# Linear attention and a gated product on one core: the projection of the last six d_ff tiles of the first token chunk in three float32r products

## The chip, the cores and the metric

The kernel runs on one core of a Trainium2 chip. The metric is the device time of one execution in microseconds, given as the median of several runs. The kernel before takes 996.69 us (three runs, 996.67 to 998.06). Smaller is better.

## What is computed

Attention without a score matrix, then a gated product of two linear layers and an output projection, all in float32:

```
q_s = softmax(q over the 64 head dims);  k_s = softmax(k over the 576 positions)
kv  = k_s^T v            (64 x 64 for each of 8 batches and 8 heads)
x   = q_s kv             (4608 tokens x 512)
out = ((x w_a) * (x w_b)) w_out      (w_a, w_b 512 x 1536, w_out 1536 x 512)
```

## The kernel before, in words

The 4608 tokens are nine chunks of T = 512. d_ff = 1536 is NF = 12 tiles of 128. Weights arrive in HBM as 64-bit words and `to_float` (L85 to L105) makes float32 of them on the chip: two ScalarE passes (L97, L98), one VectorE shift (L100), one GpSimd add (L101), one VectorE merge (L102). The result lies in one of eight buffers `wy`.

Matmuls are exact enough only if each float32 operand is written as a sum of two float32r values: `split` (L74 to L80) has ScalarE cast the source into `hi` (L77) and VectorE subtract `hi` from the source into `lo` (L80). A product then is three float32r matmuls: hi with hi, hi with lo, lo with hi.

**The first chunk (c = 0)** runs in the loop at L550 to L564, one pass for each d_ff tile f. A pass issues the loads of tile f + 3 (`load_f`), the conversion of tile f + 2 (`convert_f`: two halves of w_a and w_b, then w_out), one step of the attention of the next chunk (`attend`), then `gate_first` for tile f and the projection of tile f - 1. `gate_first` (L369 to L387) makes two PSUM tiles of 12 float32r matmuls each (L378), has ScalarE copy the first to `ga` (L385) and VectorE multiply it by the second (L386). `project_first` (L408 to L413) multiplies `ga` by w_out in plain float32: four matmuls of 128x512 (L410), which the profile shows as eight records. The float32 w_out that it reads sits in the half of `wo` that will hold `lo`; `convert_wo` (L122 to L127) brings it there with a DMA from `wy` on SP's queue (L126).

**The later chunks (c = 1 to 8)** run a seven-product scheme on 2x2 blocks (L401) and project with `project` (L415 to L423): 12 float32r matmuls of 128x512 for a tile (L420). They need w_out as hi and lo, which `split_wo` (L129) makes, in place, of the float32 copy; it is called in chunk 1 (L603, L604). The last tile of chunk 0 is projected from `run_pending` inside chunk 1.

**The order of the work.** The program order above is only the order in which the instructions are given. When the program is built, a scheduler simulates it and lays down for each engine a fixed sequence, in which an instruction can run far earlier or later than its place in the source; on the chip every engine and SP's DMA queue work their sequence in order. So the casts and subtractions of `split_wo` are not all found in chunk 1.

The edge between chunk 0 and chunk 1 matters below. Chunk 1 needs the attention output of its last head pair: PE transposes q (`pq`, L316), ScalarE and VectorE split it into `qh` and `ql` (L77, L80), PE makes `px` (L333), ScalarE copies it to `xf` (L472), VectorE and ScalarE make the operands `xt`, `xo` (L351, L77, L80), and only then can `ky` and `ka` (L401) begin.

Of the kernel before, what the change touches and what calls it, by code (L numbers as in the profile page):

```python
# [7 lines left out]
F32 = mybir.dt.float32  # L8
# [21 lines left out]
def linear_attention_then_gated_ffn(  # L30
# [17 lines left out]
    nc = tc.nc  # L48
    B, NP, P, J, _, D = k.shape
# [4 lines left out]
    T = 512  # L54
    H = T // 2
    TT = T // P
    NCH = NT // T

    const = ctx.enter_context(tc.tile_pool(name="const", bufs=1))
    sb = ctx.enter_context(tc.tile_pool(name="sb", bufs=2))  # L60
# [13 lines left out]
    def split(hi, lo, src, hi_engine="act"):  # L74

        if hi_engine == "act":
            nc.scalar.copy(out=hi, in_=src)  # L77
        else:
            nc.vector.tensor_copy(out=hi, in_=src)
        nc.vector.tensor_tensor(out=lo, in0=src, in1=hi.bitcast(F32), op=ALU.subtract)  # L80


    wo = {}

    def to_float(raw):  # L85

        top = raw.bitcast(F32).rearrange("p (n t) -> p n t", t=2)[:, :, 1]
        low = raw.bitcast(U32).rearrange("p (n t) -> p n t", t=2)[:, :, 0]
        y = sb.tile([P, DM], F32, name="wy", bufs=8)
        r = sb.tile([P, DM], I32, name="wr", bufs=4)
        u = raw.bitcast(I32)[:, 0:DM]
        nc.scalar.activation(out=y, in_=top, func=AF.Copy, scale=2.0 ** -112)  # L97
        nc.scalar.activation(out=r, in_=low, func=AF.Copy, scale=2.0 ** -29)  # L98
        yi = y.bitcast(I32)
        nc.vector.tensor_single_scalar(u, yi, 3, op=ALU.logical_shift_left)  # L100
        nc.gpsimd.tensor_tensor(out=r, in0=u, in1=r, op=ALU.add)  # L101
        nc.vector.scalar_tensor_tensor(  # L102
            out=yi, in0=yi, scalar=-(2 ** 31), in1=r, op0=ALU.bitwise_and, op1=ALU.bitwise_or
        )
        return y  # L105
# [3 lines left out]
    def load_f(f):  # L109

        i, r = divmod(f, 2)
        for half in range(2):
            raw = sb.tile([P, DM], I64, name="raw", tag="xo", bufs=11)
            ins = nc.sync.dma_start(out=raw, in_=w_ab[i, r, half])
            raws[f, half] = raw
        raw = const.tile([P, DM], I64, name=f"wo{f}_raw", tag=f"wo{f}")
        with tc.issue_after(ins.ins):
            nc.sync.dma_start(out=raw, in_=w_out[f])
        raws[f, "o"] = raw
        return ins  # L120

    def convert_wo(f):  # L122

        y = to_float(raws.pop((f, "o")))
        w = const.tile([P, 2, DM], F32R, name=f"wo{f}_w", tag=f"wo{f}")
        nc.sync.dma_start(out=w[:, 1].bitcast(F32), in_=y)  # L126
        wo[f] = w  # L127

    def split_wo(f):  # L129
        split(wo[f][:, 0], wo[f][:, 1], wo[f][:, 1].bitcast(F32))  # L130


    def ws_tile():
# [32 lines left out]
    def sums(i):  # L166

        a = {}
        for r in range(2):
            for h in range(2):  # L170
                a[r, h] = sb.tile([P, DM], F32, name="ws_y", tag="wy", bufs=8)
                nc.sync.dma_start(out=a[r, h], in_=dy[i, r, h])
        sub, add = ALU.subtract, ALU.add
        for o, x, y, op in (
            ((1, 1), (1, 0), (1, 1), add),
            ((1, 0), (0, 0), (1, 0), sub),
            ((0, 0), (1, 1), (0, 0), sub),
            ((0, 1), (0, 1), (0, 0), sub),
        ):
            nc.gpsimd.tensor_tensor(out=a[o], in0=a[x], in1=a[y], op=op)  # L180
        return {S1: a[1, 1], S3: a[1, 0], S2: a[0, 0], S4: a[0, 1]}
# [161 lines left out]
    def x_operands(xf, which, box):  # L343

        b11, b12 = xf[:, 0:2, 0:H], xf[:, 0:2, H:T]
        b21, b22 = xf[:, 2:4, 0:H], xf[:, 2:4, H:T]
        for op in which:
            if op == T2:
                t1, t2 = t_tile(), t_tile()
                nc.vector.tensor_tensor(out=t1, in0=b12, in1=b11, op=ALU.subtract)  # L350
                nc.vector.tensor_tensor(out=t2, in0=b22, in1=t1, op=ALU.subtract)  # L351
                box["t1"], box["t2"] = t1, t2
                src = t2
            elif op == T3:
                src = t_tile()
                nc.vector.tensor_tensor(out=src, in0=b22, in1=b12, op=ALU.subtract)
            elif op == T1:
                src = box["t1"]
            elif op == T4:
                src = box["t2"]  # L360
                nc.vector.tensor_tensor(out=src, in0=b21, in1=src, op=ALU.subtract)
            else:
                src = {B11: b11, B21: b21, B22: b22}[op]
            o = xo_tile([P, 2, 2, H])
            split(o[:, 0], o[:, 1], src)
            box[op] = o


    def gate_first(f, x):  # L369

        pp = []
        for n in range(2):
            pt = ps.tile([P, T], F32, name=f"pt{n}", tag=f"k{n}")
            i = 0
            for g in range(NP):
                w = blocks[f, g // 2][:, n, :, g % 2]
                for wp, xp in ((0, 0), (0, 1), (1, 0)):
                    nc.tensor.matmul(  # L378
                        pt, w[:, wp], x[g][:, xp], start=(i == 0), stop=(i == 3 * NP - 1)
                    )  # L380
                    i += 1
            pp.append(pt)
            if n == 0:
                ga = sb.tile([P, T], F32, name="ga", tag=f"gh{f % 2}", bufs=1)
                nc.scalar.copy(out=ga, in_=pt)  # L385
        nc.vector.tensor_tensor(out=ga, in0=pp[1], in1=ga, op=ALU.mult)  # L386
        return ga  # L387

    def g_split(f, g):
        gh = sb.tile([P, T], F32R, name=f"gh{f % 2}", bufs=1)  # L390
        gl = sb.tile([P, T], F32R, name=f"gl{f % 2}", bufs=1)
        split(gh, gl, g)
        return gh, gl
# [14 lines left out]
    def project_first(f, g, po):  # L408
        for t in range(TT):
            nc.tensor.matmul(  # L410
                po[t], g[:, t * P:(t + 1) * P], wo[f][:, 1].bitcast(F32),
                start=(f == 0), stop=(f == NF - 1),
            )  # L413

    def project(f, ghl, po):  # L415
        gh, gl = ghl
        for t in range(TT):
            ts = slice(t * P, (t + 1) * P)
            for i, (a, w) in enumerate(((gh, 0), (gh, 1), (gl, 0))):
                nc.tensor.matmul(  # L420
                    po[t], a[:, ts], wo[f][:, w],
                    start=(f == 0 and i == 0), stop=(f == NF - 1 and i == 2),
                )  # L423

    def store(c, po):
        for t in range(TT):
            ot = sb.tile([P, DM], F32, name="ot", tag="wr", bufs=4)
            if c == NCH - 1:
                nc.scalar.copy(out=ot[:, 0:H], in_=po[t][:, 0:H])
                nc.vector.tensor_copy(out=ot[:, H:], in_=po[t][:, H:])  # L430
            else:
                nc.scalar.copy(out=ot, in_=po[t])
            nc.sync.dma_start(out=out[c * T + t * P:c * T + (t + 1) * P, :], in_=ot)
# [83 lines left out]
    def convert_f(f):  # L517
        convert_ab(f, 0)
        convert_ab(f, 1)
        convert_wo(f)  # L520
# [27 lines left out]
    po = [ps.tile([P, DM], F32, name=f"po{t}") for t in range(TT)]  # L548
    pending = None
    for f in range(NF):  # L550
        for n in range(2, 4) if f == 0 else (f + 3,):
            if n < NF:
                last_load = load_f(n)
        if f + 2 < NF:
            convert_f(f + 2)
        if f:
            attend()
        if f == NF - 1:
            sy[0] = sums(0)
            x_operands(xfs[1], early + late, xo)  # L560
        ghl = gate_first(f, x0)
        if pending is not None:
            project_first(*pending, po)
        pending = (f, ghl)  # L564
    pend = [(pending[0], pending[1], 0, po)]

    def run_pending(last_only=False):

        if not pend:
            return  # L570
        f, ghl, c, po = pend.pop(0)
        (project if c else project_first)(f, ghl, po)
        if f == NF - 1:
            store(c, po)

    for c in range(1, NCH):
        more = c + 1 < NCH
        attend = Spread(attention_tasks(c + 1) if more else [], 3 * NI - 3)
        po = None
        x, xo = xo, {}  # L580
        for i in range(NI):
# [15 lines left out]
            u2 = sb.tile([P, 2, H], F32, name="u2", bufs=1)  # L597
# [13 lines left out]
            if more and i == NI - 1:  # L611
                x_operands(xfs[c + 1], late, xo)
            end = c == NCH - 1 and i == NI - 1
            if not end:
                run_pending()
# [11 lines left out]
            if po is None:  # L627
                po = [ps.tile([P, DM], F32, name=f"po{t}") for t in range(TT)]
# [60 lines left out]
```

## Time and profile before

| | |
|---|---|
| median of the runs | 996.69 us |
| the profiled execution's own time | 995.74 us |
| its span | 993.3 us |
| PE busy | 962.1 us (97%) |
| VectorE busy | 654.0 us (66%) |
| ScalarE busy | 333.5 us (34%) |
| granted TensorE clock, mean | 0.991 |

The span is the stretch from the first to the last instruction; 2.4 us of the execution lie around it. In the rows, PE is TensorE's matmuls, PEld its weight loads, DVE is VectorE, ACT ScalarE, POOL GpSimd, SPq SP's DMA queue. A line number is the line of the kernel before. A helper such as `split` has one line for all its callers, so tile names (`wo_w`, `gh`, `ws`, `ql`) tell them apart. Matmul records overlap, so pitches are read from the chain of work rather than from the mean duration of a record.

### The profile page before, as it was taken

What the parts mean: (1) busy time and instruction counts of PE and PEld (TensorE: products, weight loads), DVE (VectorE), ACT (ScalarE), POOL (GpSimd) and SP (SyncE); (2) the same over time, 40 slices, a digit from 0 to 9 for tenths busy, and PEclk for the clock granted to TensorE, in tenths of its full rate; (3) what the DMA queues carried; (4) which work ended last, traced back from release to release, by engine and by line L of the source; (5) the groups of instructions that cost most, each with busy time, mean ns of one, the idle gap of its engine ahead of it and who ended that gap; (6) DMA issues with size and microseconds to landing.
All of it is one profiled execution on the core that took longest, in us unless ns stands there. A gap on an engine that the chain in (4) does not pass through costs nothing.

```text
span 993.3 us, 16580 instructions
## 1 busy us (share of the span) xinstructions
PE 962.1 (97%) x6276; PEld 866.0 (87%) x6276; DVE 654.0 (66%) x1280; ACT 333.5 (34%) x667; POOL 114.2 (11%) x96
## 2 busy tenths in 40 slices
PE   4889999999999999999999999999999999999998
PEld 4667666999989999999999999999999999999996
DVE  7797887887787774677468656865577555353433
ACT  7666675332342322233223212322233232121111
POOL 3344345440000000000000000000000000000000
PEclk9799998999999999999999999999999999999999
DMA  9599858978777587866796679767867676767761
GB/s 345 216 413 401 336 213 282 384 276 294 239 272 270 212 292 270 292 220 240 239 331 228 229 249 325 257 219 245 296 221 250 211 274 216 251 238 271 252 207 50
DMA packets 84605, 261.35 MB, mean 263 GB/s; under 512 B 9392, under 2 KB 9520, under 8 KB 84528
## 3 DMA queue, kind: packets, MB, share of 16 engines
q1 hardware_dynamic: 84528, 260.31, 73.8%
q8 instruction: 50, 0.82, 0.3%
q14 instruction: 27, 0.22, 0.1%
HBM read 219.38 MB, written 37.75 MB: 259 GB/s over the span
## 4 chain that ended last, share of the span: by engine, by line
PE 83%; DVE 4%; DMA 4%; issue 3%; ACT 2%; POOL 2%; SPq 0%; POOLq 0%; DVEq 0%; ACTq 0%
PE po L420 26%; PE ka L401 14%; PE kx L401 14%; PE kp L401 14%; PE ky L401 7%; PE pk L249 3%; PE px L333 2%; POOL wr L101 2%; PE pt L378 2%; PE po L410 1%; DMA wo_w<-wy 1%; PE pq L316 1%; DMA wo_raw<-in_w_out 1%; DVE ws L80 1%; DMA qt<-in_q 1%
## 5 line engine op out<-in xcount | busy, mean ns | idle before, releaser
L420 PE MATMUL po<-wo_w,gh 128*128 128x512 f32 x768 | 225.0, 394 | 1.0 <-ACT gh L77 1.0
L401 PE MATMUL kx<-xo,ws 128*128 128x256 f32 x1152 | 167.1, 285 | 0.0
L401 PE MATMUL ka<-xo,ws 128*128 128x256 f32 x1152 | 161.9, 285 | 0.2 <-ACT xo L77 0.2
L420 PEld LDWEIGHTS po<-wo_w,gh 128*128 128x128 f32 x768 | 138.4, 189 | 26.6 <-ACT gh L77 1.4
L401 PE MATMUL kp<-xo,ws 128*128 128x256 f32 x1152 | 157.4, 284 | 0.0
L401 PEld LDWEIGHTS kx<-xo,ws 128*128 128x128 f32 x1152 | 152.4, 191 | 4.0 <-ACT ws L77 0.2
L401 PEld LDWEIGHTS ka<-xo,ws 128*128 128x128 f32 x1152 | 151.3, 192 | 4.3 <-ACT xo L77 0.7
L401 PEld LDWEIGHTS kp<-xo,ws 128*128 128x128 f32 x1152 | 147.2, 191 | 1.6
L420 PE MATMUL po<-wo_w,gl 128*128 128x512 f32 x384 | 136.8, 397 | 0.0
L77 ACT CAST gh<-cc 128x512 fp32r<-128x512 f32 x96 | 58.7, 622 | 159.1 <-DVE cc L632 113.1
L631 DVE TENSOR_TENSOR cc<-kp,u 128x512 f32<-128x512 f32 x48 | 33.0, 687 | 82.3 <-PE kp L401 81.9
L420 PEld LDWEIGHTS po<-wo_w,gl 128*128 128x128 f32 x384 | 71.1, 189 | 14.8
L401 PE MATMUL ky<-xo,ws 128*128 128x256 f32 x576 | 80.1, 288 | 1.0 <-ACT xo L77 1.0
L378 PE MATMUL pt<-xo,ws 128*128 128x512 f32 x288 | 74.1, 406 | 3.9 <-ACT ga L385 3.2
L401 PEld LDWEIGHTS ky<-xo,ws 128*128 128x128 f32 x576 | 73.8, 194 | 1.6 <-ACT xo L77 1.4
L80 DVE TENSOR_TENSOR gl<-cc,gh 128x512 fp32r<-128x512 f32 x96 | 68.0, 714 | 10.1 <-ACT gh L77 10.1
L622 ACT COPY cc<-kx 128x256 f32<-128x256 f32 x48 | 17.9, 372 | 168.3 <-PE kx L401 162.9
L621 DVE TENSOR_TENSOR cc<-kp,u 128x512 f32<-128x512 f32 x48 | 33.0, 688 | 62.2 <-PE kp L401 61.9
L378 PEld LDWEIGHTS pt<-xo,ws 128*128 128x128 f32 x288 | 53.3, 188 | 20.3 <-ACT ga L385 4.6
L217 POOL PARTITION_ALL_REDUCE mx<-m x20 | 14.7, 733 | 475.1 <-DVE m L203 434.8
L410 PE MATMUL po<-wo_w,ga 128*128 128x512 f32 x96 | 43.5, 592 | 0.0
L635 DVE TENSOR_TENSOR cc<-ka,u 128x512 f32<-128x512 f32 x48 | 32.9, 685 | 15.4 <-PE ka L401 15.2
(119 smaller groups left out, 1211.0 us busy)
## 6 DMA issues: line engine op xcount, KB each, us to landing
ws<-dw SPq DMA_DIRECT2D x312, 512.0 KB, 4.7
dw<-ws SPq DMA_DIRECT2D x42, 512.0 KB, 4.7
raw<-in_w_ab SPq DMA_DIRECT2D x24, 512.0 KB, 7.9
out<-ot SPq DMA_DIRECT2D x36, 256.0 KB, 4.1
vt<-in_v SPq DMA_DIRECT2D x28, 325.0 KB, 6.1
qt<-in_q SPq DMA_DIRECT2D x32, 256.0 KB, 4.0
kt<-in_k SPq DMA_DIRECT2D x24, 320.0 KB, 4.6
wo_raw<-in_w_out SPq DMA_DIRECT2D x12, 512.0 KB, 8.1
```

Source lines behind the costliest of these rows:

```text
L77: nc.scalar.copy(out=hi, in_=src)
L80: nc.vector.tensor_tensor(out=lo, in0=src, in1=hi.bitcast(F32), op=ALU.subtract)
L101: nc.gpsimd.tensor_tensor(out=r, in0=u, in1=r, op=ALU.add)
L249: nc.tensor.matmul(pk, kt[:, j].rearrange("p h d -> p (h d)"), vt[:, j], start=(j == 0), stop=(j == J - 1),)
L333: nc.tensor.matmul(px[:, s], w, m[:, s], start=(i == 0), stop=(i == 2))
L378: nc.tensor.matmul(pt, w[:, wp], x[g][:, xp], start=(i == 0), stop=(i == 3 * NP - 1))
L401: nc.tensor.matmul(pt[:, n], w[:, n, wp, c], x[:, xp, c], start=(first and n == 0 and i == 0), stop=(i == 5), skip_group_check=True,)
L410: nc.tensor.matmul(po[t], g[:, t * P:(t + 1) * P], wo[f][:, 1].bitcast(F32), start=(f == 0), stop=(f == NF - 1),)
L420: nc.tensor.matmul(po[t], a[:, ts], wo[f][:, w], start=(f == 0 and i == 0), stop=(f == NF - 1 and i == 2),)
L621: nc.vector.tensor_tensor(out=cc[:, 3], in0=kp, in1=u3, op=ALU.add)
L631: nc.vector.tensor_tensor(out=cc[:, 1], in0=kp, in1=u2, op=ALU.add)
L635: nc.vector.tensor_tensor(out=cc[:, 2], in0=ka, in1=u2, op=ALU.add)
```

## The change

With F0 = 6, tiles f = 6 to 11 of the first chunk go another way. Their w_out is split straight from `wy` when it is converted, so there is no float32 copy and no DMA for it; `split_wo` does nothing for them. Their gate result goes into a buffer shared with `u2` and is then split with `g_split` into `gh` and `gl`; their projection is `project`, three float32r products, in place of `project_first`. Tiles 0 to 5 stay as they were.

```diff
+    F0 = 6
...
         y = to_float(raws.pop((f, "o")))
         w = const.tile([P, 2, DM], F32R, name=f"wo{f}_w", tag=f"wo{f}")
-        nc.sync.dma_start(out=w[:, 1].bitcast(F32), in_=y)
+        if f < F0:
+            nc.sync.dma_start(out=w[:, 1].bitcast(F32), in_=y)
+        else:
+            split(w[:, 0], w[:, 1], y)
         wo[f] = w
 
     def split_wo(f):
-        split(wo[f][:, 0], wo[f][:, 1], wo[f][:, 1].bitcast(F32))
+        if f < F0:
+            split(wo[f][:, 0], wo[f][:, 1], wo[f][:, 1].bitcast(F32))
...
             if n == 0:
-                ga = sb.tile([P, T], F32, name="ga", tag=f"gh{f % 2}", bufs=1)
+                ga = sb.tile([P, T], F32, name="ga", tag=f"gh{f % 2}" if f < F0 else "u2", bufs=1)
                 nc.scalar.copy(out=ga, in_=pt)
         nc.vector.tensor_tensor(out=ga, in0=pp[1], in1=ga, op=ALU.mult)
-        return ga
+        return ga if f < F0 else g_split(f, ga)
...
         if pending is not None:
-            project_first(*pending, po)
+            (project_first if pending[0] < F0 else project)(*pending, po)
         pending = (f, ghl)
...
         f, ghl, c, po = pend.pop(0)
-        (project if c else project_first)(f, ghl, po)
+        project(f, ghl, po)
```

## Rows read from the trace of the kernel before

**Rows 1.** The page: busy time by engine, and two of the costliest groups.
```profile
PE 962.1 (97%) x6276; PEld 866.0 (87%) x6276; DVE 654.0 (66%) x1280; ACT 333.5 (34%) x667; POOL 114.2 (11%) x96
...
L77 ACT CAST gh<-cc 128x512 fp32r<-128x512 f32 x96 | 58.7, 622 | 159.1 <-DVE cc L632 113.1
...
L80 DVE TENSOR_TENSOR gl<-cc,gh 128x512 fp32r<-128x512 f32 x96 | 68.0, 714 | 10.1 <-ACT gh L77 10.1
```

**Rows 2.** Busy time of each engine in four stretches; first column the stretch, then its length.
```profile
95.00:147.00 52.00, 50.84 (x198) 34.85 (x197) 42.52 (x69) 35.01 (x85) 22.41 (x16) 1.00 0.73 280
147.00:157.00 10.00, 10.00 (x42) 7.17 (x41) 4.59 (x8) 3.90 (x9) 6.15 (x5) 1.00 0.86 310
157.00:177.00 20.00, 17.54 (x78) 12.69 (x77) 19.20 (x30) 11.90 (x21) 10.41 (x7) 0.83 0.85 300
161.00:263.00 102.00, 98.97 (x673) 90.43 (x671) 85.59 (x161) 37.73 (x67) 29.48 (x20) 0.97 0.86 309
```

**Rows 3.** Who waited for whom, engine PE, 90 to 178 us.
```profile
PE px L333 <- DVE ql L80: 1.7, 2, 0.9
PE ky L401 <- ACT xo L77: 1.0, 1, 1.0
PE pm L208 <- ACT xf L472: 0.7, 1, 0.7
```

**Rows 4.** The chain that ended last, 126 to 172 us: start, length, what.
```profile
137.57 3.43 PE po L410 x8
...
156.76 3.43 PE po L410 x8
...
164.35 0.60 DVE wo_w L80
...
165.48 0.69 DVE ql L80
...
166.21 1.23 PE px L333 x6
...
169.48 0.58 PE ky L401
```

**Rows 5.** The same chain in chunk 1, 188 to 200 us.
```profile
191.97 3.72 PE po L420 x16
```

**Rows 6.** The tile wo_w, 90 to 170 us: durations min/median/max in ns, first and last start.
```profile
L80 DVE TENSOR_TENSOR wo_w<-wo_w x9: 642/679/692, 95.5 to 166.7; 128x512 fp32r<-128x512 f32 x9
L77 ACT CAST wo_w<-wo_w x8: 604/614/626, 99.2 to 148.4; 128x512 fp32r<-128x512 f32 x8
L126 SPq DMA_DIRECT2D wo_w<-wy x6: 471/476/476, 95.8 to 144.0; - x6
...
DMA to landing us min/median/max: 2.3/4.2/7.5
```

**Rows 7.** Groups by line and shape, engine DVE, 95 to 147 us.
```profile
L80 DVE TENSOR_TENSOR ws<-wy,ws 128x512 fp32r<-128x512 f32 x10 | 12.0, 1201 | 2.1 <-ACT ws L77 2.1
...
L80 DVE TENSOR_TENSOR wo_w<-wo_w 128x512 fp32r<-128x512 f32 x6 | 4.0, 675 | 0.0
```

**Rows 8.** The timeline of DVE and PE: the last weight split, an idle time, tile 11's gate.
```profile
145.01 1.53 DVE L80 TENSOR_TENSOR ws<-wy,ws 128x512 fp32r<-128x512 f32 x1
...
154.20 0.69 DVE L299 TENSOR_REDUCE qst<-qt 128x8 f32<-128x512 f32 x1 [3.13 <-DMA qt<-in_q]
...
149.78 4.21 PE L378 MATMUL pt<-xo,ws 128*128 128x512 f32 x16
```

**Rows 9.** Busy time by stretch at the edge of chunk 0; third number from the end the clock.
```profile
168.00:170.00 2.00, 0.85 (x2) 0.43 (x2) 1.92 (x4) 1.24 (x4) 0.00 (x0) 0.62 0.94 357
170.00:172.00 2.00, 1.98 (x10) 1.92 (x10) 2.00 (x6) 1.78 (x5) 0.00 (x0) 0.50 1.04 412
172.00:174.00 2.00, 2.00 (x11) 2.00 (x11) 2.00 (x5) 1.05 (x2) 0.84 (x1) 0.50 1.05 410
174.00:176.00 2.00, 2.00 (x14) 2.00 (x13) 2.00 (x4) 0.22 (x1) 1.92 (x2) 0.68 1.04 400
```

## The prediction, made before the changed kernel was run

> **What bounds the kernel now.** I began with the page's busy times [rows 1]: PE is busy 97% of the span, so PE is the first suspect everywhere. Since an average hides stages, I then read the busy times of the stages that the change touches [rows 2]. From 95 to 147 us, where tiles 6 to 10 are gated, PE is busy 50.84 of 52 us; DVE is busy 42.52, so 9.48 us of it are idle. From 157 to 177 us, the edge between the first and the second chunk, the picture turns: DVE is busy 19.20 of 20 us and PE only 17.54. After the edge PE is the bound again (98.97 of 102 us, chunk 1).
>
> The waits of PE [rows 3] say the same in another way. From 90 to 178 us PE loses 1.7 us in two waits for `ql`, 1.0 for `xo` and 0.7 for `xf`, nearly all of it at the edge, and almost nothing before. The chain of work that ended last [rows 4] shows what such a wait hangs on: the last head pair's `ql` runs at 165.48 us right behind other DVE work, a w_out subtraction at 164.35 among it; `px` follows at 166.21 and `ky` at 169.48. So a microsecond of PE work saved before about 165 us arrives at the end only if this chain moves forward with it.
>
> **The change part by part.**
>
> *The product, on the path.* A plain float32 projection takes 3.43 us for its eight records [rows 4]. In chunk 1, 16 float32r records of the same 128x512 take 3.72 us, 0.2325 each [rows 5], so the twelve of `project` take 2.79 us. That is 3.43 - 2.79 = 0.64 us less for a tile, and for tiles 6 to 11 it is 6 x 0.64 = 3.8 us off PE, all of it in stretches where PE is the bound (the first of the six runs after 119 us, the last right before the edge's `px`).
>
> *The gate split, added.* Six casts of 0.62 us on ACT and six subtractions of 0.71 us on DVE [rows 1]. A projection comes one whole gate and one other projection later than its own gate (24 and 12 records of 0.23 us, 5.5 + 2.8 us), and the added multiply-cast-subtract chain is 0.7 + 0.62 + 0.71, about 2 us, plus its queueing; I cost the latency at nothing, hidden by the next gate. If DVE and ACT queues ate those 8 us, PE would wait. ACT has 17 us idle of 52 in the stage [rows 2] and takes the casts easily.
>
> *The w_out splits, moved.* The view of `wo_w` [rows 6] shows that the scheduler already runs these casts early (99.2 to 148.4 us), so ACT gains little extra work. The DVE subtractions overwrite what `project_first` reads and so trail each projection, up to 166.7 us. In the changed kernel they can run right at conversion, where the DMA was issued (95.8 to 144.0 us). Inside 95 to 147 us DVE gets three more of them (nine, for tiles 3 to 11, in place of the six for tiles 3 to 8, [rows 6, 7]) and four gate subtractions: seven. At 0.68 us, the mean of the `wo_w` row [rows 7], that is 4.8 us. At 1.20 us, the mean of the `ws` subtractions of the same shape in the same stage [rows 7], it is 8.4 us. Both fit into the 9.48 us that DVE has idle, the second barely. I take the lower end as nearer, since the `wo_w` row is the moved operation itself, and cost it at nothing on PE while weights stay ahead. The cover is thin: the last weight split ends at 145.01 + 1.53 = 146.54 us, PE starts tile 11's gate at 149.78 [rows 8] and needs that half of the weights six records of 0.23 us, 1.4 us, later. With 4 x 0.64 us saved before it, PE would want them at about 148.6 us, 2 us after they are there now.
>
> A rule bears on this price. The two subtraction rows differ by 0.53 us although shape and engine are the same, and POOL is busy 22.41 of the 52 us [rows 2]. The Trainium skill, "SBUF — State Buffer", section "Who interferes with whom", says that a VectorE instruction with two SBUF inputs contends with a GpSimd instruction that reads SBUF, and that the loser blocks fully. By it every added subtraction can be held by the weight conversion's GpSimd add; the sum would go by the 8.4 us.
>
> *The DMAs, removed.* Six transfers of w_out and their issues leave SP's queue (0.48 us each; 4.2 us to landing, [rows 6]). They hold a `wy` buffer until they land; instead a cast and a subtraction hold it. Nothing on PE waits for them, so I count 0; it works against any lateness of the conversions. What may go wrong with queues: the cast of w_out now stands on ACT straight behind the DVE merge, and whatever follows on ACT waits with it; the shared single buffer for `ga` makes ACT's copy for the next tile wait for the subtraction of this one, but a whole half gate, 2.7 us, lies between.
>
> *The edge.* This is the unknown. Upper bound of the gain: `ql` no longer stands behind the w_out subtraction (0.60 us) and PE's wait for it (0.7) vanishes, so the whole 3.8 us pass and about 0.7 more, 4.5. Lower bound: the DVE sequence from 157 us keeps its pace, because its inputs (a q load that lands at 154.2, [rows 8], and sums on POOL) don't move with PE; then `ql` is earlier by the subtraction alone, 0.6 us. I take 3.2 us, nearer the upper end: the chain starts on PE with the transpose `pq`, which moves with PE, and DVE sits idle 3.13 us ahead of 154.2 and for 5.4 of the 10 us from 147 to 157 [rows 8, 2], so it has room to begin early.
>
> **Sum.** The profiled execution took 995.74 us (span 993.3 and 2.4 around it). 995.74 - 3.2 = 992.5 for it; the median of the runs lies 0.95 us above that execution, so 996.69 - 3.2 = 993.5 us is the number. About 0.2%, 2.0 us, is what a measurement of this kernel can tell from no change: faster means under 994.7, slower over 998.7.
>
> **The rivals.**
>
> *B. The edge swallows it.* DVE holds the edge; only the subtraction that leaves it is gained: 996.69 - 0.6 = 996.1. For it: DVE 19.20 of 20 us busy there. Against: idle DVE right before, and a fresh order by the scheduler. Between B and the forecast the gain is a matter of degree.
>
> *C. Slower: the conversions come late.* DVE gets its seven subtractions at 1.20 us or more between 95 and 147 us, they stand in front of merges and weight splits, and tiles 10 and 11 wait on PE for `ws`. Up to 2 us of lateness is free; the 3.8 us saved are used up at 5.8 us of lateness, and past that it is a loss. If PE idles there for a few microseconds, the clock can fall as it did at the edge, where after PE's waits the granted clock went to 0.50 of full speed, its lower level of 1.2 GHz, for 170 to 174 us [rows 9]. That stretch cost PE's busy time times the missing clock: 0.85 x 0.38 + 1.98 x 0.50 + 2.00 x 0.50 + 2.00 x 0.32 = 3.0 us. 8 us of lateness (2.2 lost) with half of such a fall gives 996.69 + 2.2 + 1.5 = 1000.4; without it 998.9. The rule of the skill named above speaks for this one, the thin 2 us of slack too; against it that the added work at either price fits into DVE's idle time and six DMAs go.
>
> *D. The clock stays up at the edge.* If the new order closes PE's waits there, the 3.0 us of [rows 9] come back on top: 996.69 - 3.2 - 3.0 = 990.5. Against it: PE comes earlier to the same chain, which rather lengthens its waits.
>
> *E. No cheaper product* (the float32r records running slower with freshly made operands) is excluded by [rows 5], the same tile, form and operands; no chance of its own.
>
> **How the numbers follow.** Forecast 0.47, B 0.25, C 0.16, D 0.12. Faster is the forecast and D, 0.59; same is B, 0.25; slower is C, 0.16. The range goes from 990.3, which takes in D, to 997.0, which takes in B and half a microsecond for the spread of the runs; C stays outside. The forecast's own range, by the two ends of the edge short of B, is 992.2 to 994.9.
>
> **What would show it.** Right: in the changed profile each of six projections of 12 float32r records takes about 2.8 us; PE waits for nothing new from 95 to 157 us; tile 11's gate begins about 2.5 us earlier; `ky` of chunk 1 begins near 166.3 instead of 169.48; from there to the end all is shifted by the same 3.2 us. B shows as an unchanged start of `ky` with longer waits on `ql` or `xo`. C shows as PE waiting for `ws` between 130 and 155 us behind subtractions that last over a microsecond. D shows as a clock of 1.00 through the edge. Wrong in another way: a new order of the later chunks that moves the end although the edge stands where I put it.

## The result and the profile after

The changed kernel takes 1001.55 us (median of 5 runs, 999.87 to 1002.75) against 997.04 for the kernel before on the same chip: a ratio of 1.0045 (95% interval 1.0032 to 1.0059). It is slower, by 4.5 us, where 993.5 had been forecast. The profiled execution took 999.87 us, with a span of 997.9.

The page's busy times answer to [rows 1], the busy times by stretch (same columns) to [rows 2], the waits of PE from 90 to 178 us to [rows 3]:

```profile
PE 961.3 (96%) x6300; PEld 872.4 (87%) x6300; DVE 661.1 (66%) x1286; ACT 336.1 (34%) x673; POOL 118.4 (12%) x96
```

```profile
95.00:147.00 52.00, 45.88 (x190) 33.98 (x189) 48.01 (x70) 33.64 (x67) 22.70 (x15) 0.97 0.66 252
147.00:157.00 10.00, 10.00 (x48) 8.15 (x47) 5.09 (x10) 6.19 (x27) 5.20 (x4) 1.00 0.72 259
157.00:177.00 20.00, 16.82 (x82) 13.82 (x81) 16.41 (x26) 12.00 (x23) 10.21 (x8) 0.88 0.64 232
...
112.00:114.00 2.00, 0.00 (x0) 0.00 (x0) 2.00 (x3) 1.44 (x4) 0.66 (x1) 1.00 0.64 251
114.00:116.00 2.00, 1.53 (x4) 1.24 (x5) 2.00 (x5) 2.00 (x4) 0.00 (x0) 0.50 0.71 283
116.00:118.00 2.00, 2.00 (x8) 1.58 (x7) 2.00 (x2) 1.87 (x4) 1.67 (x1) 0.65 0.85 261
```

```profile
PE px L338 <- DVE ql L81: 3.8, 3, 1.9
PE pt L383 <- DVE ga L391: 2.5, 1, 2.5
PE ky L406 <- ACT xo L78: 1.0, 1, 1.0
PE po L425 <- DVE gl L81: 0.8, 1, 0.8
PE pm L213 <- ACT xf L477: 0.7, 1, 0.7
```

From 95 to 147 us PE is now busy 45.88 of 52 us (50.84 before), and DVE 48.01 (42.52 before). DVE's 5.49 us more lie inside what had been predicted, 4.8 to 8.4, and they fit into its idle time; PE lost 5 us all the same. Part of that agreement is luck. DVE's groups of the changed kernel in this stretch give what the added subtractions cost:

```profile
L81 DVE TENSOR_TENSOR wo_w<-wy,wo_w 128x512 fp32r<-128x512 f32 x6 | 5.2, 860 | 0.0
...
L81 DVE TENSOR_TENSOR gl<-ga,gh 128x512 fp32r<-128x512 f32 x3 | 4.0, 1327 | 0.5 <-ACT gh L78 0.5
...
L81 DVE TENSOR_TENSOR wo_w<-wo_w 128x512 fp32r<-128x512 f32 x3 | 3.1, 1042 | 0.0
```

These twelve take 12.3 us where six took 4.0 [rows 7]: 8.3 us for six more. DVE's busy time rose by less because PE and the conversions run later, so that less of DVE's other work falls into the stretch.

The waits say what PE stood still for in this stretch: once for `ga` (2.50 us) and twice for `ql` (1.86 and 1.33 us; the third wait for `ql`, 0.60 us, is at the edge). The timeline of DVE and PE shows the first of them, and the projection of one tile:

```profile
107.73 1.75 DVE L81 TENSOR_TENSOR ws<-wy,ws 128x512 fp32r<-128x512 f32 x1
109.41 1.51 DVE L101 TENSOR_SCALAR raw<-wy 128x512 int32<-128x512 int32 x1
110.84 2.37 DVE L103 SCALAR_TENSOR_TENSOR wy<-wy,wr 128x512 int32<-128x512 int32 x2
113.13 0.68 DVE L81 TENSOR_TENSOR ws<-wy,ws 128x512 fp32r<-128x512 f32 x1
113.73 0.68 DVE L391 TENSOR_TENSOR ga<-pt,ga 128x512 f32<-128x512 f32 x1
...
114.47 4.36 PE L383 MATMUL pt<-xo,ws 128*128 128x512 f32 x12 [2.50 <-DVE ga L391]
...
130.87 0.62 PE L425 MATMUL po<-wo_w,gh 128*128 128x512 f32 x2
...
133.65 2.43 PE L383 MATMUL pt<-xo,ws 128*128 128x512 f32 x10
...
159.06 1.09 PE L383 MATMUL pt<-xo,ws 128*128 128x512 f32 x4
...
161.64 5.17 DVE L81 TENSOR_TENSOR ws<-ws_y,ws 128x512 fp32r<-128x512 f32 x3
166.74 0.68 DVE L81 TENSOR_TENSOR gl<-ga,gh 128x512 fp32r<-128x512 f32 x1
...
168.54 0.68 DVE L81 TENSOR_TENSOR ql<-pq,qh 128x512 fp32r<-128x512 f32 x1
...
172.53 0.58 PE L406 MATMUL ky<-xo,ws 128*128 128x256 f32 x1 [1.05 <-ACT xo L78]
```

Three things are to be seen. A projection of twelve float32r records takes 133.65 - 130.87 = 2.78 us, as predicted. The multiply of tile 6 (`ga`, 113.73) stands on DVE behind weight conversions of 1.5 to 1.75 us each, so PE waits 2.50 us, does nothing from 112 to 114, and then works at a granted clock of 0.50 and 0.65, the lower level of 1.2 GHz in part: its twelve records take 4.36 us, where twelve at full clock took 3.00 at 108.96. And at the edge three `ws` subtractions (5.17 us together) stand ahead of `gl` and `ql`; `ky` starts at 172.53, 3.05 us later than before [rows 4].

The edge did not make that delay, though. In the kernel before, the last records of tile 11's gate were these:

```profile
154.76 2.00 PE L378 MATMUL pt<-xo,ws 128*128 128x512 f32 x8
```

They ended at 156.76; in the changed kernel they end at 160.15 (159.06 + 1.09), 3.39 us later. From there to `ky` it takes 12.38 us, before 12.72. PE had ended the gate of tile 6 ahead (105.34 against 106.28): the time went between the two gates.

The subtractions that last 1.7 us in place of 0.68 do so beside additions on POOL. The Trainium skill, "SBUF — State Buffer", section "Who interferes with whom", says that a VectorE instruction with two SBUF inputs contends with a GpSimd instruction that reads SBUF, that the ports they share are an exclusive lock, and that the one that comes second is blocked. The trace agrees: the subtraction at 107.73 took 1.75 us against 0.68 for the same shape, and it ended 0.53 us behind POOL's addition (109.48 against 108.95).

**Where the time went, in one sum.** From each profiled execution's trace I added, after the first 45 us, the gaps between PE's records (idle) and PE's busy time in each slowed stretch times the missing share of the clock (lost to the clock); what is left is PE's own work at full clock, and about 4 us behind PE's last record that are much the same in all of them (3.95 to 4.27). A stretch is slowed where the granted clock is below 1.00.

| profiled execution | span | PE idle | lost to the clock | PE's work | first `ky` |
|---|---|---|---|---|---|
| before | 993.3 | 10.3 | 2.9 | 935.1 | 169.5 |
| after | 997.9 | 15.4 | 6.3 | 931.3 | 172.5 |

PE's work fell by 3.8 us, the predicted product term (executions with the same product differ by up to 3 us in this column, as a table further down shows; where that comes from was not traced). Idle time rose by 5.1 and the clock's loss by 3.4: -3.8 + 5.1 + 3.4 = 4.7, against 997.9 - 993.3 = 4.6. So the gain is real; the question is why PE waits longer. The same sums by stage say where, each cell idle and, behind the stroke, lost to the clock:

| stage | before | after |
|---|---|---|
| 45 to 95 us | 3.0 / 0 | 2.2 / 0 |
| to the end of tile 11's gate | 1.2 / 0 | 6.1 / 1.5 |
| to the first `ky` | 2.4 / 0 | 3.2 / 0 |
| to 300 us | 2.8 / 2.9 | 2.3 / 4.8 |
| to the end | 1.0 / 0 | 1.6 / 0 |

Nearly all of the added idle time lies ahead of the edge, in the stages of tiles 6 to 11.

### The profile page after: what moved, and what is told of

Its sections match the earlier page's. It is cut to its first block, busy times and chain, and to the rows that moved or that the text cites. A ratio compares the mean times of both kernels' runs of the same rounds, so it can differ in the third digit from the quotient of the medians.

```text
span 997.9 us, 16624 instructions
## 1 busy us (share of the span) xinstructions
PE 961.3 (96%) x6300; PEld 872.4 (87%) x6300; DVE 661.1 (66%) x1286; ACT 336.1 (34%) x673; POOL 118.4 (12%) x96
## 4 chain that ended last, share of the span: by engine, by line
PE 82%; DVE 2%; DMA 1%; ACT 1%; issue 1%; SPq 0%; DVEq 0%; ACTq 0%
PE po L425 27%; PE ka L406 14%; PE kp L406 14%; PE kx L406 13%; PE ky L406 7%; PE pk L254 3%; PE px L338 2%; PE pq L321 1%; PE pt L383 1%; DMA qt<-in_q 1%; DVE ws L81 0%; DVE wy L103 0%; ACT ot L437 0%; DVE xt L356 0%; DVE qt L305 0%
## 5 line engine op out<-in xcount | busy, mean ns | idle before, releaser
L425 PE MATMUL po<-wo_w,gh 128*128 128x512 f32 x816 | 238.7, 394 | 1.0 <-ACT gh L78 1.0
L425 PEld LDWEIGHTS po<-wo_w,gh 128*128 128x128 f32 x816 | 147.2, 189 | 28.2 <-ACT gh L78 1.4
L425 PE MATMUL po<-wo_w,gl 128*128 128x512 f32 x408 | 144.8, 396 | 0.8 <-DVE gl L81 0.8
L425 PEld LDWEIGHTS po<-wo_w,gl 128*128 128x128 f32 x408 | 75.2, 188 | 16.6 <-DVE gl L81 1.3
L81 DVE TENSOR_TENSOR gl<-cc,gh 128x512 fp32r<-128x512 f32 x96 | 66.0, 691 | 9.8 <-ACT gh L78 9.8
L228 ACT ACTIVATE kt<-kt 128x640 f32<-128x640 f32 x24 | 17.8, 740 | 79.4 <-DVE kt L225 76.9
```

What stands on the lines that cost most here:

```text
L228: nc.scalar.activation(out=kf, in_=kf, func=AF.Exp)
L425: nc.tensor.matmul(po[t], a[:, ts], wo[f][:, w], start=(f == 0 and i == 0), stop=(f == NF - 1 and i == 2),)
```

## The experiments

Three theories were weighed: that the added split work on DVE costs it; that the edge swallows the gain (rival B of the prediction), plus something else for the loss; that the scheduler, given a changed program, lays down another order, and the order is worse. The record of each run stands ahead of it. "Low parts left out" means that in the projections of the first chunk's last six tiles one operand stands for both parts of the gate, of w_out or of both, as the text says: the number of matmuls is kept, but what is multiplied in place of the low part is the same operand again, so the output isn't that of the kernel. This holds for e1, e2, e3, e5, e8, e11, e13 and e14. Ratios are to the kernel before on the same chip.

### Which part: one at a time, in the scheduler's own order

Twelve float32r products with nothing split (the product alone; the low parts of the gate and of w_out are left out), then with the gate split, then with the early w_out split, then the whole change for three tiles:

```diff
 e1:  ga = sb.tile([P, T], F32 if f < F0 else F32R, ...)      (cast in the multiply, no split)
-         po[t], a[:, ts], wo[f][:, w],
+         po[t], a[:, ts], wo[f][:, 1 if first else w],
 e2:  e1's second edit alone, the gate split as in the change
 e3:  e1's first edit alone, w_out split as in the change
 f0_9:
-    F0 = 6
+    F0 = 9
```

> The cheaper product alone: tiles 6 to 11 of chunk 0 are projected in twelve float32r records, but nothing is split for it (the gate result is written once as float32r and stands for both parts, the copied w_out stands for both parts; w_out is split in chunk 1 as before). Left out: the low parts of the first chunk's last six projections. Theory Q (VectorE's queue became the bound from 105 us on, by the added subtractions): with none of them PE keeps its 3.8 us, so 993 to 994.5 against 997.0, no wait of PE over 1 us between 95 and 160 us. Rival O (the scheduler's fresh order of the queues is what lost the time, whatever the load): this kernel is reordered too and lands anywhere, 997 or above as likely as not. Rival P (the product itself gives nothing): 996 to 998.

> Product and gate split, with w_out as in the kernel before (copied by DMA, split late; the copy stands for both parts in the product). Left out: the split of w_out for the first chunk's last six projections. Theory Q: four gate subtractions more in the 95 to 147 us stretch, three fewer w_out subtractions than in the changed kernel: about half of the 8.3 us between the ends is lost, 996 to 998.5 against 997.0, waits of PE on ga or ql shorter than in the changed kernel. Rival S (the one buffer that ga shares with u2, and the longer chain behind the gate, stop ScalarE and PE): as slow as the changed kernel, 1000 to 1002. Rival O: anywhere.

> Product and the early split of w_out, with the gate result unsplit (written once as float32r, it stands for both parts; two alternating buffers as before). Left out: the low part of the gate result in the first chunk's last six projections. Theory Q: three more subtractions in the stretch, though straight at conversion, where VectorE's order is tightest: 996 to 999 against 997.0. Rival S (the gate's buffer and chain): back to 993 to 995, since the buffer and chain are gone. Rival O: anywhere.

> The changed kernel with F0 = 9: only tiles 9, 10 and 11 go the new way. The product gives 3 x 0.64 = 1.9 us. Theory Q: their gate subtractions come after 137 us, where VectorE soon has idle time, and their w_out subtractions after 125 us; a small loss of 0 to 1.5 us, so 995 to 997 against 997.0, and no wait on ga near 112 us. Rival O: no order by the number of tiles; 1000 or more is possible. Rival S: half of the loss stays, about 999.

Measured: e1 1001.39 us, 1.0044 (1.0027 to 1.0060); e2 1003.53, 1.0063 (1.0046 to 1.0081); e3 999.78, 1.0028 (1.0017 to 1.0039); f0_9 1003.20, 1.0061 (1.0045 to 1.0077). The product alone, with no split added anywhere, is as slow as the whole change. And more parts do not mean more time: the whole change for three tiles (f0_9) takes as long as the product with the gate split for six (e2). So added DVE work can't be the whole cause. Nor can the shared buffer and the longer chain of theory S (e2), which e1 has not. But an equal time does not mean the same cause: e1's PE ends tile 11's gate at 153.38 and starts `ky` at 168.57, 3.4 and 0.9 us ahead of the kernel before, and loses its time from the end of that gate to 300 us. One thing is tied to a part: the timeline of e3 has the stalls of the changed kernel near 115 and 122 us,

```profile
115.32 3.06 PE L383 MATMUL pt<-xo,ws 128*128 128x512 f32 x12 [2.46 <-DVE ga L394]
122.52 0.30 PE L338 MATMUL px<-qh,kvh 128*128 128x64 f32 x1 [3.01 <-DVE ql L81]
```

and e1, e2 and f0_9, where w_out is converted as before in those tiles, have no wait over 1.3 us there. That stall comes with the early w_out splits.

### Work and order apart

The same programs were then held to a given order: each engine's instructions, SP's DMAs too, are chained one behind the other by ordering edges that carry no semaphore. e5 is the product alone in the order of the kernel before; e6 is the kernel before, unchanged, in the order that the scheduler had laid down for e1; e7 is the whole change in the order of before, each w_out split 1.2 us (cast) and 2.6 us (subtraction) behind its conversion, each gate split 0.3 and 1.5 us behind its multiply.

```diff
+def keep_order(nc, tc, glued):
...
+    for e, packed in ORDER.items():
...
+        flat = [i for u in order for i in units[e][u]]
+        for a, b in zip(flat, flat[1:]):
+            tc.add_manual_dep(b, a.name, info, reason="order")
```

> The work of e1 (the cheaper product alone, its low parts left out), but every engine and SP's queue are held to the order that they have in the kernel before, by ordering edges; in each of the six projections three float32r matmuls stand where one float32 matmul stood. Theory O (the fresh order lost the time): the 3.8 us come through nearly whole, 993 to 994.5 against 997.1, and PE's waits at the two edges (near 166 and 280 us) no longer than in the kernel before by more than 1 us. Theory B (what feeds the edges does not move with PE, whatever the order): 996 to 998, PE's waits at the edges longer by what was saved.

> The opposite: the work of the kernel before, unchanged, with every engine held to the order that the scheduler gave e1. Theory O: an order that costs e1 about 8 us against its own work costs this one as well; 1000 to 1006 against 997.1, with the long waits on ql and xf near 165 and 280 us and the clock's falls there. Theory B: the plain product brings PE to the edges as late as before, so the waits are short and the time is that of the kernel before, 996 to 998.

> The whole change, in the order of the kernel before: the six w_out splits put about 1.2 us (ScalarE) and 2.6 us (VectorE) behind their conversion, the six gate splits 0.3 and 1.5 us behind the gate's multiply, everything else as before. Theory O: 993 to 995.5 against 997.1, faster than both kernels. Theory Q, what is left of it (VectorE's added work makes its queue late even in a good order): 998 to 1001, with PE waiting on ga or ql between 110 and 125 us. Theory B: 996 to 998.

Measured: e5 998.08 us, 1.0008 (0.9997 to 1.0019); e6 1002.04, 1.0049 (1.0036 to 1.0063); e7 1000.43, 1.0028 (1.0017 to 1.0039).

| | order of before | order laid down for e1 |
|---|---|---|
| float32 product | 1 | 1.0049 (e6) |
| float32r product | 1.0008 (e5) | 1.0044 (e1) |

Read down, the cheaper product gains little or nothing. In the old order the interval of e5 (0.9997 to 1.0019) leaves room for 0.03%, which excludes the 3.8 us; in the order of e1 the intervals of e6 and e1 leave room for some 2 us. Read across, the new order alone costs 0.4 to 0.5%, with not one instruction changed. So e6 agrees with the theory that the order costs (1000 to 1006), and e5 lies just above the range of rival B (996 to 998). e7 fell where the theory of the added load had put it (998 to 1001): in the old order, too, the added splits cost time, 0.20% against e5, though the intervals overlap. Where the new order costs time stands in the timeline of e6: waits at the first edge, and again a little later in chunk 1, that the kernel before doesn't have:

```profile
168.11 0.30 PE L367 MATMUL px<-qh,kvh 128*128 128x64 f32 x1 [1.93 <-DVE ql L114]
...
188.95 1.70 PE L435 MATMUL ky<-xo,ws 128*128 128x256 f32 x12 [0.89 <-DVE cc L665]
```

Why the product is worth nothing shows in the chain of work that ended last, of e5, from 155 us (start, length, what):

```profile
155.61 1.72 POOL ws_y L216
...
157.35 0.63 ACT ws L112
...
158.00 1.12 DVE ws L115
159.12 1.18 DVE qst L342
...
162.52 1.75 DVE qt L344
...
166.54 0.61 DVE ql L115
...
167.20 2.08 PE px L369 x6
...
171.31 0.58 PE ky L440
```

No projection stands in this stretch of it. PE is free for `px` at 162.74, 2.75 us sooner than before (165.49), but `px` starts at 167.20 and not at 166.21. It waits 4.46 us for `ql`, where it waited 0.72 before: 3.74 us more, about the product's saving. `pq` ended on PE near 159 us, and ACT and DVE could have made `qh` and `ql` at once; but on DVE `ql` stands behind `ws` subtractions that wait for sums on POOL, and behind a 1.75 us multiply. POOL's sums begin at 152.88; in the kernel before, with PE later, they begin at 151.74, both times when a load has landed. They don't come sooner when PE does. That is rival B.

### Giving the edge way

If so, the product must pay once `ql` stands elsewhere. e8 is e5 with two instructions moved; e10, the control, is the kernel before with the same move; e9 is e7 with it and with the earlier `qh` and `ql`, for which PE waited at 118.5 us, moved as well.

```diff
 the order on ACT                      the order on DVE
  L112 ws<-ws_y x3                      L342 qst
+ L112 qh<-pq                         + L115 ql<-pq,qh
  L112 ws<-ws_y                         L115 ws<-ws_y x2, L344 qt, L115 wo_w, ws
- L112 qh<-pq                         - L115 ql<-pq,qh
```

> As e5_product_old_order (twelve float32r products, nothing split, the low parts of gate and w_out left out; the order of the kernel before), with two instructions moved: the last qh cast of the first chunk stands ahead of the fourth of the ws casts on ACT, and its ql subtraction ahead of the second ws subtraction, the reciprocal and the 1.75 us multiply on DVE. Theory B1 (the edge swallowed the cheaper product because ql stands on DVE behind work that is paced by POOL's sums): ql is done near 161 us in place of 167.15, px starts when PE is free near 163 us, the 4.46 us wait goes, ky starts 2.5 to 4 us earlier (167.3 to 168.8) and the median is 994 to 995.5. Theory B2 (the sums and the last w_in conversions themselves hold the edge, whoever stands ahead of them): the wait for ql goes, but a wait for ws or xo takes its place, ky stays within 1 us of 171.3 and the time within 1 us of 998.1.

> Control: the kernel before, in its own order, with the same two instructions moved and the float32 product kept. Theory B1: PE is busy with the projections until 165.5 us, so the place of ql can give back only its 0.72 us wait there: 996.3 to 997.3. If the move of ql alone is worth 2.5 us or more without the cheaper product (994.5 or less), then what e8 gains is not the product's.

> As e7_change_old_order (the whole change, nothing left out), with the same move of the last ql, and with the qh cast and ql subtraction that held PE 2.07 us at 118.5 us moved ahead too (qh ahead of a w_in cast near 111 us, ql ahead of a 1.5 us subtraction near 113 us). Theory B1: both waits (2.07 and 3.39 us) go with the clock lost behind them, what is left is the cheaper product less the 0.7 us wait for qt: 993.5 to 995.5, faster than both kernels. Theory R (the added splits cost DVE more than the order can give back): another wait for ga, gl or ws comes up on PE between 105 and 172 us and the time stays at 997.5 or more.

Measured: e8 995.61 us, 0.9990 (0.9980 to 1.0000); e10 998.05, 1.0014 (1.0001 to 1.0027); e9 998.68, 1.0017 (1.0008 to 1.0026). With the move the product is worth 1.0014 - 0.9990 = 0.24%, 2.4 us (by the intervals some 1.6 us either way); without it, it was worth nothing that can be told. Against the kernel before, e8 is ahead by 0.10%, 1.1 us, and its interval reaches 1.0000; a part of the 2.4 us is the wait of the control that is shown below and that e8 doesn't have. The timeline of e8 shows how far it went:

```profile
160.53 0.69 DVE L115 TENSOR_TENSOR ql<-pq,qh 128x512 fp32r<-128x512 f32 x1
...
163.86 1.76 DVE L344 TENSOR_TENSOR qt<-qt,qst 128x512 f32<-128x512 f32 x1
...
167.95 0.68 DVE L387 TENSOR_TENSOR xt<-xf,xt 128x512 f32<-128x512 f32 x1
...
163.15 0.19 PE L369 MATMUL px<-qh,kvh 128*128 128x64 f32 x1
...
169.33 0.58 PE L440 MATMUL ky<-xo,ws 128*128 128x256 f32 x1 [3.45 <-ACT xo L112]
```

`ql` is done 5.9 us earlier than in e5 and `px` starts 4.05 us earlier with no wait. Then `xt` stands behind the same DVE work, `ky` waits 3.45 us for `xo` and comes only 2.0 us earlier. The time is 0.1 us above what the first theory gave (994 to 995.5), and the place of `ky` (expected up to 168.8, measured 169.33) is half-way to the second: what was late next took about half.

The control missed its number (996.3 to 997.3) on the slow side. Its edge is passed sooner, `ky` at 168.59 against 169.48; its timeline shows the gain given back 12 us on:

```profile
180.24 1.69 PE L435 MATMUL kx<-xo,ws 128*128 128x256 f32 x12 [1.87 <-DVE cc L657]
...
178.03 0.69 DVE L333 TENSOR_REDUCE qst<-qt 128x8 f32<-128x512 f32 x1 [2.00 <-DMA qt<-in_q]
```

A reduction that stands on DVE ahead of `cc` waits for a load of q that lands at 178.0. That load was issued at 171.08 us, 1.2 us later than in the kernel before (169.86), where it landed at 177.7; PE, being early, now feels it. Being chained as such costs little here: from the first `ky` of the fourth chunk to PE's last record e10 takes 503.5 us, and so does the kernel before.

e9 missed the forecast of the first theory (993.5 to 995.5) and came out where the theory that the added splits cost too much had put it (997.5 or more): its ratio fell from e7's 1.0028 to 1.0017, about 1.1 us, and the intervals overlap.

### What is late next

e11 is e8 with `xt` (L387, L392) moved on DVE ahead of the multiply L344 and the `wo_w` subtractions, `xf` on ACT ahead of two `ot` copies, and the reduction L335 behind the sums of `cc`. e12 is e9 with these moves and two copies of `ga` on ACT moved ahead of a conversion step each.

```diff
 the order on DVE (e11 against e8)
+ L115 ws<-ws_y x2, L387 xt, L392 xt
  L344 qt, L115 wo_w
- L115 ws<-ws_y x2
  L115 wo_w
- L387 xt, L392 xt
```

> As e8_product_early_ql (only the cheaper product, low parts left out), with what was late next moved too: on DVE the two xt additions stand right behind the last two ws subtractions and ahead of the 1.75 us multiply of qt and the two wo_w subtractions, on ACT the copy of xf stands ahead of two ot copies, and behind the edge the reduction that waits for a q load stands behind the sums of cc. Theory B1 (each step of the edge stands behind work in a fixed order on DVE, so the product's gain comes through piece by piece as that order gives way): the wait of ky for xo falls from 3.45 us to 1.0 to 2.0 us, ky starts at 167 to 168, no wait on cc, and the median is 993 to 994.5, with a span near 991.5 to 992.5. Theory B2 (the conversions of ws, paced by POOL's sums, hold the edge): ky waits for ws near 169 us, whoever stands ahead, and the time stays within 0.7 us of 995.6.

> As e9_change_early_ql (the whole change, nothing left out), with the moves of e11_product_early_x and, on ACT, the two copies of ga that held PE 1.53 and 1.56 us near 120 and 130 us moved ahead of the integer-to-float steps they stood behind. Theory B1: both ga waits and the cc wait go, ky starts at 167.5 to 169, and the median falls by 3 to 5 us from 998.68, to 993.5 to 995.5, below the kernel before. Theory R (the twelve added split steps cost DVE and ACT more than an order can give back): other waits take their place and it stays at 996.7 or more.

Measured: e11 996.39 us, 0.9990 (0.9979 to 1.0002); e12 999.14, 1.0016 (1.0005 to 1.0027). The median of e11 missed the first theory, and so did that of e12, which fell where the other theory had put it (996.7 or more). The edge itself gave way as expected in e11, to 166.91, 2.6 us ahead of the kernel before; the end did not follow:

```profile
166.91 0.39 PE L440 MATMUL ky<-xo,ws 128*128 128x256 f32 x1 [1.79 <-ACT xo L112]
...
169.47 2.71 PE L440 MATMUL ky<-xo,ws 128*128 128x256 f32 x11 [1.37 <-DVE xo L115]
```

From `ky` to the first `ky` of the next chunk it takes 115.7 us, against 112.4 before. The next `xo` is late (1.37 us), and the profiled execution lost 6.0 us to the clock, e8's only 1.8. In e12 a wait of 3.00 us for the multiply of `ga` came up at 143.02. Each move opened the next wait.

### Which split

> As e8_product_early_ql, with the six gate splits (a cast on ACT, a subtraction on DVE) added behind the multiply of each tile; w_out converted as in the kernel before, and its low part left out of the first chunk's projections. The whole change in this order (e9_change_early_ql, e12_change_early_x) stood 0.27% above e8 and e11. Theory G (the gate splits cost it, as the multiply and the projection of a tile now wait for one more step of ACT and of DVE): 1.0012 to 1.0020 of the kernel before, with waits of po for gl or of pt for ga that e8 doesn't have. Theory W (the moved w_out subtractions cost it): within 0.1% of e8, 0.998 to 1.000.

> As e8_product_early_ql, with the six w_out splits moved ahead into the conversion of each tile and the gate not split (its low part left out). Theory W: 1.0012 to 1.0020 of the kernel before, with waits of pt for ga or of px for ql between 105 and 150 us that e8 doesn't have. Theory G: within 0.1% of e8, 0.998 to 1.000. If both kernels lie half-way, near 1.0005, the two splits share it.

```diff
 e13: e8 and the gate splits
+        pair = split(gh, gl, g)
 e14: e8 and the early w_out splits
+            split(w[:, 0], w[:, 1], y)
```

Measured: e13 999.25 us, 1.0021 (1.0012 to 1.0031); e14 998.00, 1.0010 (0.9997 to 1.0023). The gate splits cost 0.31% against e8, intervals apart; that is the price of all six. For the w_out splits it is 0.20%, but the intervals touch (0.9980 to 1.0000 for e8). By the expectations e13 lies just above theory G (1.0012 to 1.0020 where the gate splits cost it), and e14 between the two theories, which leaves the share of the w_out splits open. The two don't add up to e9 (1.0017) either, whose earlier `ql` stands elsewhere. Where the gate splits come in on the path, in the timeline of e13:

```profile
162.30 1.77 DVE L120 TENSOR_TENSOR gl<-ga,gh 128x512 fp32r<-128x512 f32 x1
163.99 1.26 DVE L347 TENSOR_SCALAR qst<-qst 128x8 f32<-128x8 f32 x1
165.17 0.68 DVE L120 TENSOR_TENSOR ql<-pq,qh 128x512 fp32r<-128x512 f32 x1
...
164.12 0.50 PE L463 MATMUL po<-wo_w,gl 128*128 128x512 f32 x1 [0.83 <-DVE gl L120]
...
172.13 0.58 PE L444 MATMUL ky<-xo,ws 128*128 128x256 f32 x1 [3.48 <-ACT xo L117]
```

The last `gl` takes 1.77 us beside POOL and is one more link ahead of `ql`, `xt` and `xo`: `ky` starts 2.8 us later than in e8 (169.33). But 2.0 of the 2.8 us are there before it, at the reduction that waits for a load of q, here in e13 and then in e8:

```profile
156.88 0.69 DVE L340 TENSOR_REDUCE qst<-qt 128x8 f32<-128x512 f32 x1 [3.05 <-DMA qt<-in_q]
```

```profile
154.84 0.69 DVE L335 TENSOR_REDUCE qst<-qt 128x8 f32<-128x512 f32 x1 [4.28 <-DMA qt<-in_q]
```

The load was issued at 151.82 us in e13 and at 149.62 in e8; tile 11's gate, too, ends 2.2 us later (158.19 against 155.95). So the last `gl` can have added about 0.8 us; the rest was there before it.

### Seven of the profiled executions side by side

| profiled execution | span | PE idle | lost to the clock | PE's work | first `ky` |
|---|---|---|---|---|---|
| e6, before's work, e1's order | 1002.0 | 16.5 | 5.4 | 935.1 | 171.4 |
| e10, before's work, early `ql` | 995.0 | 12.9 | 1.7 | 935.4 | 168.6 |
| e1, product alone | 997.6 | 14.5 | 8.2 | 929.8 | 168.6 |
| e5, product, before's order | 997.5 | 15.9 | 7.5 | 929.1 | 171.3 |
| e8, with early `ql` | 993.5 | 15.1 | 1.8 | 931.6 | 169.3 |
| e7, whole change, before's order | 998.8 | 14.3 | 8.2 | 931.3 | 174.5 |
| e13, e8 and gate splits | 999.0 | 17.4 | 4.3 | 932.2 | 172.1 |

PE's work is 935 us with the float32 product and 929 to 932 with the other, in whatever order. In no row is that gain lost by slower matmuls: the other differences are PE's waits and the clock. Where the spread from 929 to 932 comes from was not traced. Each row is one execution, up to 2 us from the median of its kernel (e5's took 999.88 us, its median is 998.08), so single rows are not to be set against each other to a microsecond.

## Why the prediction was wrong

**The product term held.** 0.64 us for a tile and 3.8 us in all: 2.78 us for a projection, and 935.1 - 931.3 = 3.8 in the sum. Two other steps failed. The first is where the trace of the changed kernel shows its loss; the second alone would have left the time where it was.

**"Cost it at nothing on PE" failed for the added subtractions, those of w_out above all.** They were put at their lower end, 4.8 us, because the `wo_w` row "is the moved operation itself"; measured are 8.3 us, as several of them ran beside POOL's additions. And the step forgot what stands behind them. DVE works its queue in order, so what counts is how much stands ahead of the instruction that PE waits for, and not whether the sum fits into idle time. From 95 us to the end of tile 11's gate PE waits 6.1 us in place of 1.2, for `ga` of tile 6 and for `ql`, and loses 1.5 us to the clock. e3 ties the first two of these waits to the early w_out splits (2.46 and 3.01 us in e3; 1.3 at most in e1, e2 and f0_9). How much of the loss is the added work and how much the order that the scheduler gave it is not settled (below). The signs that the prediction had named fail in the same place: "PE waits for nothing new from 95 to 157 us", tile 11's gate 2.5 us earlier (it begins 3.8 us later, at 153.58), `ky` near 166.3 (172.53). The rows before had shown the spot: the 1.7 us of waits for `ql` [rows 3] were read as lying nearly all at the edge, but only 0.72 of them does; the rest stands where the changed kernel lost its time, here in the kernel before:

```profile
116.57 0.30 PE L333 MATMUL px<-qh,kvh 128*128 128x64 f32 x1 [0.94 <-DVE ql L80]
```

Rival C had the direction, and its times (998.9 to 1000.4) were the nearest, but it looked for late `ws` of tiles 10 and 11; what was late were `ga` and `ql`, behind conversions and splits.

**The edge failed as well: "I take 3.2 us".** The prediction chose a value near the upper end because the chain starts with `pq` on PE and DVE sits idle before. e5, with the product alone in the old order, shows the lower end or less: 3.74 us more of waiting for `ql`, no gain. The evidence had been named (the q load that lands at 154.2, the sums on POOL) and set against the idle time of DVE; but that idle time was itself the wait for that load. An engine that is idle because its next instruction in order waits for a transfer has no room to begin early. Rival B had this mechanism, with a chance of 0.25; its 996.1 is near e5 and not near the changed kernel, which loses ahead of the edge too.

**"Hidden by the next gate" failed for the last gate split.** Behind tile 11 no gate follows: its projection waits 0.83 us for `gl` at 167.47. e13 prices all six gate splits at 0.31% in the order of e8; of the 2.8 us by which `ky` is late there, 2.0 come before the last of them.

**The new order was seen as a mark and not as a price.** "A new order of the later chunks" was one line without a chance. e6 shows that an order alone can cost 0.49%. How the 0.45% of the changed kernel divide can be read along one path: product in the old order 0.08%, both splits 0.20% more (e7), its own order 0.17% more. The last step's intervals overlap, and e6 shows the price of e1's order, not of this one, so that share isn't settled. In the later chunks the new order is dear by little: from 300 us on PE idles 1.6 us in place of 1.0, and the clock loses nothing.

**The clock** was right as a mechanism (half clock behind a wait), and it fell in more places: 6.3 us lost in place of 2.9, 1.5 of them ahead of the edge.

No run beats both kernels. e8 and e11 are 0.1% below the kernel before, intervals at or over 1, and leave the low parts out; the best whole change, e12 with 1.0016 or e9 with 1.0017, stays above it.

## What to carry to other kernels

A microsecond saved on the busiest engine counts only as far as the next place where that engine waits: follow the chain back from that wait, and if it runs through a transfer, or another engine that doesn't depend on the saved work, the saving can be worth nothing there. Idle time ahead of an instruction that waits for a transfer is no slack for what stands behind it. Where a scheduler lays down the order, compare the changed program in the old order too before the difference is put down to the change.

## What was not expected of the hardware

The clock doesn't always fall behind the same wait. In eight profiled executions (before, after, e1, e5, e6, e8, e11, e13) PE waits some 2.2 us for `ga` near 71 us, and the clock falls behind that wait in three (e1, e5, e11). Timeline of PE, in e8 and then in e11, whose orders are the same up to there:

```profile
71.64 3.04 PE L414 MATMUL pt<-xo,ws 128*128 128x512 f32 x12 [2.17 <-ACT ga L421]
```

```profile
71.54 4.61 PE L414 MATMUL pt<-xo,ws 128*128 128x512 f32 x12 [2.15 <-ACT ga L421]
```

The same twelve records take 3.04 us in the one and 4.61 in the other, 1.6 us more; from 72 to 74 us the granted clock is 1.00 in the first and 0.50 in the second. Runs of one kernel on this chip spread over 4 us or so (the kernel before: 994.2 to 998.9 us in 29 runs), and such falls may be a part of it; that was not tried.

An instruction of 128x8 elements on DVE (L347 of e13) took 1.26 us beside POOL's sums, where the same step took 0.15 us at 169.14 in the changed kernel, with POOL idle: what it lost there was not set by its own size.
